# The last store of a recurrence-and-mixture kernel, cut into four uneven parts, and two pairs of stores merged

## The chip, the cores and the metric

The kernel runs on one core of one Trainium2 chip. Its time is the device time of one execution in microseconds (us). The core has a tensor engine (PE, with its weight loads shown as PEld), a vector engine (DVE), a scalar engine (ACT), GpSimd (POOL), a sync engine (SP) that here only issues DMAs, and 16 DMA engines that move the data.

## The reference

Two layers follow each other. The first is a gated recurrence over 5056 tokens for 4 sequences of 256 channels; the second is a soft mixture of 8 experts with 4 slots each, over all 4 x 5056 = 20224 tokens.

```python
# x, f_logit: (4, 5056, 256) f32; lower_bound: (256,)
f = lower_bound + (1 - lower_bound) * sigmoid(f_logit)
for t in range(S):
    h = f[:, t] * h + (1 - f[:, t]) * x[:, t]
    y[:, t] = h
x = y.reshape(B * S, D)
# phi: (256, 32); w1: (8, 256, 1024); w2: (8, 1024, 256)
logits = x @ phi
d = softmax of logits over all tokens        # dispatch
slot_input = d.T @ x                         # 32 x 256
slot_out[e] = relu(slot_input[e] @ w1[e]) @ w2[e]
c = softmax of logits over the 32 slots      # combine
out = c @ slot_out                           # (20224, 256) f32
```

The output has 20.7 MB. No row of it can be computed before `slot_out` is there, and that needs all tokens.

## The kernel before

The kernel has three stages. Until about 130 us it streams `f_logit` and `x` through the recurrence in groups of 512 tokens and keeps the exponentials of the logits (`etall`, slots on the partitions) and the slot sums. Until 143 us the experts' two products give `slot_out` and `slot_bd` (two copies of it, each masked for one of two sequences). Then the output stage combines and stores.

In the output stage the tokens of a sequence are cut into blocks: two of 2048 tokens and one of 896 (`blocks`; `end = len(blocks) - 1` is the index of the small one), and 64 left-over tokens. Within a block, partition p holds n_r tokens in a row (16 or 7), so that a partition's part of a store is contiguous in the output: 16 tokens of 1 KB are one run of 16 KB. `whole` (L786) computes one sequence's block by itself. `couple` (L801) computes a block for the two sequences 2j and 2j + 1: for each token position r one matmul (L811) with `slot_bd` into PSUM, then a scaling by 1 / row sum that moves it into the tile `ob`, on ACT (L816) where r % 7 is 1, 4 or 6 and on DVE (L819) otherwise. When the positions up to one of `ends` are done, they are stored through SP's queue: either both sequences in one DMA (`both`, L828) or one DMA for each (L831). `rest` (L835) does the left-over tokens.

The order of the stage is written out by hand at the end (L853 to L862): sequence 3's first block in four stores, the small block for sequences 0 and 1 (`couple(end, 0, (4, 7))`) and for 2 and 3 (`couple(end, 1)`), sequence 2's first block, the left-over tokens, and then three couples of large blocks: `couple(0, 0)`, `couple(1, 0)`, `couple(1, 1)`. Each of these six sequences' blocks is a store of 128 partitions x 16 KB = 2048 KB. The last one, sequence 3's second block, is the last store of the kernel.

The stores stand in SP's program in that order, and SP issues each when the results that it stores are there. Each DMA on SP's queue also takes one of eight semaphores in turn, so an issue waits for the landing of the DMA eight before it. DMAs on GpSimd's queue have semaphores of their own. In the expert stage that queue carries the weights; in the output stage GpSimd does nothing after the two `slot_bd` instructions (L747). The tile `phi_f` (L68), which the change writes to, is loaded at L81 and read by `phi_constants` (L117) near the start.

Of the kernel before, what the change touches and what calls it, by code (L numbers as in the profile page):

```python
# [18 lines left out]
def kernel(  # L19
# [10 lines left out]
    nc = tc.nc  # L30
    B, S, D = x.shape
# [4 lines left out]
    P = 128  # L36
# [31 lines left out]
    phi_f = consts.tile([P, DC, NS], F32, name="phi_f")  # L68
# [95 lines left out]
    with tc.tile_pool(name="sp2", bufs=3) as sp2, \  # L164
# [324 lines left out]
        for n in range(n_unit):  # L489
# [16 lines left out]
            else:  # L506
                end = n >= n_unit - 6
# [108 lines left out]
    with tc.tile_pool(name="ew", bufs=1) as ew, \  # L616
# [36 lines left out]
        for q in range(E // Q):  # L653
# [4 lines left out]
            if q == 0:  # L658
                nc.tensor.matmul(cs_ps, rep2, cs1, start=True, stop=True)
                src = ht_ps.rearrange("p f (j s) -> p f j s", s=NS)[:, :, :, ds(0, SPE)]  # L660
                src = bass.AP(tensor=src.tensor, offset=src.offset,
                              ap=[list(src.ap[0]), [P, FC], [NS + SPE, Q], [1, SPE]])
                dst = hid[:, :, :, ds(0, SPE)]
                dst = bass.AP(tensor=dst.tensor, offset=dst.offset,
                              ap=[list(dst.ap[0]), [Q * NS, FC], [NS + SPE, Q], [1, SPE]])
# [4 lines left out]
            for j in range(Q):  # L670
                s0 = (Q + j) * SPE
                src = ht_ps[:, :, ds(j * NS + s0, SPE)]
# [33 lines left out]
        for j in range(Q):  # L706
# [30 lines left out]
            if j == 1:  # L737
                row_sums(25, n_grp * R)
                q = n_grp * R - 1
                k = ds(wide_r * B, (q - wide_r) * B + B // 2)  # L740
# [7 lines left out]
        for r in range(DIR):  # L748
# [3 lines left out]
            else:  # L752
# [3 lines left out]
                out=out[ds((B - 1) * S, P * wide_r)].rearrange(  # L756
                    "(p r) d -> p r d", r=wide_r)[:, r], in_=begun[:, r])
# [3 lines left out]
    with tc.tile_pool(name="osb", bufs=3, reuse_waits="tile") as osb:  # L761

        def by_vector(ob, op, scale):
            nc.vector.tensor_tensor(ob, op, scale.broadcast_to(list(ob.shape)), ALU.mult)  # L764

        def by_scalar(ob, op, scale):
            for i in range(ob.shape[1]):
                nc.scalar.activation(ob[:, i], op[:, i], ACT.Copy, scale=scale[:, i])

        def share(op, i, b, r, k):  # L770
            t0, n_r = blocks[i]
            ew = etall[ds(b * NS, NS), ds(t0, P * n_r)].rearrange("s (p r) -> s p r", r=n_r)
            for j in range(k):
                nc.tensor.matmul(op[:, j], ew[:, :, r + j], slot_out[ds(b * NS, NS)],  # L774
                                 start=True, stop=True, skip_group_check=True)

        def scale_of(i, b, r, k):
            return rrow[:, ds(blocks[i][0] // P + r, k), ds(b, 1)]

        def rows_of(i, b):  # L780
            t0, n_r = blocks[i]
            return out[ds(b * S + t0, P * n_r)].rearrange("(p r) d -> p r d", r=n_r)

        pout = ctx.enter_context(tc.tile_pool(name="pout", bufs=8, space=PSUM, reuse_waits="tile"))

        def whole(i, b, pieces, ends):  # L786
            n_r = blocks[i][1]
            dst = rows_of(i, b)
            ob = osb.tile([P, n_r, D], F32, name="ob", tag="ob")
            done = pieces[0][1]  # L790
            for j, r, k in pieces:
                op = pout.tile([P, 2, D], F32, name="op", tag="op")
                share(op, i, b, r, k)
                (by_vector, by_scalar)[j](ob[:, ds(r, k)], op[:, ds(0, k)],
                                          scale_of(i, b, r, k))
                if r + k in ends:
                    q = ds(done, r + k - done)
                    nc.sync.dma_start(out=dst[:, q], in_=ob[:, q])
                    done = r + k

        def couple(i, j, ends=()):  # L801
            t0, n_r = blocks[i]
            ends = ends or (n_r,)
            ew = etall[ds(j * 2 * NS, 2 * NS), ds(t0, P * n_r)].rearrange(
                "s (p r) -> s p r", r=n_r)
            scale = rrow[:, ds(t0 // P, n_r), ds(2 * j, 2)]
            ob = osb.tile([P, 2, n_r, D], F32, name="oc", tag="oc")
            done = 0
            for r in range(n_r):
                op = pout.tile([P, 2, D], F32, name="op", tag="op")  # L810
                nc.tensor.matmul(op.rearrange("p u d -> p (u d)"), ew[:, :, r],  # L811
                                 slot_bd[ds(j * 2 * NS, 2 * NS)].rearrange("s u d -> s (u d)"),
                                 start=True, stop=True, skip_group_check=True)
                if r % 7 in (1, 4, 6):
                    for u in range(2):
                        nc.scalar.activation(ob[:, u, r], op[:, u], ACT.Copy,  # L816
                                             scale=scale[:, r, ds(u, 1)])
                else:
                    nc.vector.tensor_tensor(  # L819
                        ob[:, :, r], op,  # L820
                        scale[:, r].unsqueeze(2).broadcast_to([P, 2, D]), ALU.mult)
                if r + 1 in ends:
                    q = ds(done, r + 1 - done)
                    if done or i == end and ends == (n_r,):
                        both = out[ds(2 * j * S, 2 * S)].rearrange(
                            "(u t) d -> u t d", u=2)[:, ds(t0, P * n_r)].rearrange(
                            "u (p r) d -> p u r d", r=n_r)
                        nc.sync.dma_start(out=both[:, :, q], in_=ob[:, :, q])  # L828
                    else:
                        for u in range(2):  # L830
                            nc.sync.dma_start(out=rows_of(i, 2 * j + u)[:, q],  # L831
                                              in_=ob[:, u, q])
                    done = r + 1

        def rest():  # L835
            n_p = B // 2
            ob = osb.tile([P, n_p, D], F32, name="ob", tag="ob")
            dst = out.rearrange("(b t) d -> t b d", b=B)
            for j in range(n_p):
                k = ds(j * 2 * NS, 2 * NS)  # L840
                op = pout.tile([P, 2, D], F32, name="op", tag="op")
                nc.tensor.matmul(op.rearrange("p u d -> p (u d)"),
                                 left[k].rearrange("s t u -> s (t u)"),
                                 slot_bd[k].rearrange("s u d -> s (u d)"),
                                 start=True, stop=True, skip_group_check=True)
                nc.scalar.copy(ob[:, j], op[:, 0])
                nc.vector.tensor_tensor(ob[:, j], ob[:, j], op[:, 1], ALU.add)
            by_vector(ob, ob, rrow[:, n_grp * R - 1, ds(0, n_p)].unsqueeze(2))
            for j in range(n_p):
                nc.sync.dma_start(out=dst[ds(S - L, L), ds(2 * j, 2)], in_=ob[:, j])  # L850

        end = len(blocks) - 1
        whole(0, B - 1, ((0, 2, 1), (1, 3, 1), (0, 4, 2), (1, 6, 2), (0, 8, 2),  # L853
                         (1, 10, 2), (0, 12, 2), (1, 14, 2)), (4, 6, 10, 16))
        couple(end, 0, (4, 7))
        couple(end, 1)
        whole(0, B - 2, [(t % 2, 2 * t, 2) for t in range(wide_r // 2)], (wide_r,))
        rest()
        for i in range(end):
            for j in range(B // 2):  # L860
                if i or j < B // 2 - 1:
                    couple(i, j)  # L862
# [30 lines left out]
```

## Time and profile before

| what | value |
|---|---|
| median of 3 runs | 197.45 us (197.3 to 197.46) |
| the profiled execution | 197.19 us, its span 195.4 us |
| busy: PE, DVE, ACT, POOL | 80%, 75%, 72%, 53% of the span |
| bytes read from HBM, written to it | 58.23 MB, 20.71 MB |
| first store issued | 143.60 us |
| last store: issued, last landing | 176.96 us, 194.50 us |
| stores of 2048 KB from L831: issue to landing, median of the six | 13.1 us |

The span runs from the first to the last instruction of the profiled execution; the time of the execution is a little longer than its span. A DMA is split into packets, one for each contiguous run, which the DMA engines work off in order; each engine ends its share with a 4-byte packet that steps the semaphore. Landing times are those of these steps. The trace gives start, duration, size and queue of each packet, but not the number of the DMA engine.

### The profile page before, as it was taken

How to read it: one execution, taken by the hardware profiler on the slowest of the kernel's cores; microseconds unless marked ns; L12 is line 12 of the kernel's file. 1: busy time of each engine (PE TensorE's matmuls, PEld its weight loads, DVE VectorE, ACT ScalarE, POOL GpSimd, SP SyncE). 2: the span in 40 equal slices, each digit the busy share in tenths (PEclk: the TensorE clock that was granted, in tenths of full speed). 3: DMA queues.
4: the chain of work that ended last, by engine and by line, in shares of the span. 5: the costliest groups of instructions: out<-in, count | busy, mean ns of one | idle time of the engine just before them, and what ended most of it. 6: DMA issues, size and time to landing. Idle time of an engine off the chain costs nothing.

```text
span 195.4 us, 3269 instructions
## 1 busy us (share of the span) xinstructions
PE 155.5 (80%) x1204; PEld 106.2 (54%) x1204; DVE 146.9 (75%) x188; ACT 140.0 (72%) x194; POOL 103.7 (53%) x80
## 2 busy tenths in 40 slices
PE   5768888999979879889797887999999999990000
PEld 4446666776767757668586575567874433320000
DVE  2679797999797999999999999815189798770000
ACT  3688698799788998989987597545279987771000
POOL 2589578874996879874979969384030000000000
PEclk9999999999997999999999999999995555555555
DMA  5999999999999999999999999999949999999995
GB/s 206 421 419 418 431 424 426 428 428 355 376 426 423 429 317 421 429 416 346 363 420 419 260 211 214 215 214 215 166 150 424 424 454 429 429 429 429 429 429 218
DMA packets 14274, 70.75 MB, mean 362 GB/s; under 512 B 1570, under 2 KB 2851, under 8 KB 10291
## 3 DMA queue, kind: packets, MB, share of 16 engines
q1 hardware_dynamic: 11632, 62.13, 76.6%
q0 software_dynamic: 2624, 8.42, 21.6%
q8 instruction: 9, 0.15, 0.3%
q14 instruction: 7, 0.05, 0.1%
q10 hardware_dynamic: 2, 0.00, 0.0%
HBM read 58.23 MB, written 20.71 MB: 404 GB/s over the span
## 4 chain that ended last, share of the span: by engine, by line
PE 33%; DVE 24%; DMA 15%; ACT 8%; issue 7%; POOL 3%; ACTq 0%; SPq 0%; DVEq 0%; POOLq 0%
DVE h L318 18%; DMA x_t<-in_x_dram 15%; PE op L811 11%; DVE ht L348 4%; PE hp L331 4%; POOL u_t L247 3%; ACT oc L816 3%; PE up L272 2%; ACT a L300 2%; PE op L774 2%; PE so_ps L712 2%; PE sp L262 2%; PE lg L362 2%; PE tail L396 1%; PE slot_ps L413 1%
## 5 line engine op out<-in xcount | busy, mean ns | idle before, releaser
L247 POOL TENSOR_TENSOR u_t<-s_t,x_t 128x1024 bf16<-128x1024 bf16 (+1 forms) x39 | 82.5, 2127 | 23.5 <-ACT s_t L236 11.1
L318 DVE TENSOR_TENSOR_SCAN h<-a,h,up 128x512 bf16<-128x512 f32 (+1 forms) x72 | 86.5, 1251 | 6.1 <-PE up L272 5.0
L236 ACT ACTIVATE s_t<-f_t 128x2048 bf16<-128x2048 f32 (+2 forms) x23 | 38.3, 1669 | 6.0 <-DMA f_t<-in_f_logit_dram 3.7
L331 PE MATMUL hp<-base,h 128*128 128x128 f32 (+1 forms) x160 | 29.1, 305 | 10.2 <-DVE ht L348 8.1
L331 PEld LDWEIGHTS hp<-base,h 128*128 128x128 f32 (+1 forms) x160 | 22.6, 207 | 20.0 <-DVE ht L348 12.7
L811 PE MATMUL op<-slot_bd,etall 64*128 64x512 bf16 x62 | 26.2, 596 | 0.8 <-DVE ob L764 0.2
L300 ACT ACTIVATE a<-sp,lbs 128x1024 f32<-128x1024 bf16 x24 | 25.4, 1113 | 1.5 <-PE sp L262 1.0
L816 ACT ACTIVATE oc<-op,rrow 128x256 f32<-128x256 f32 x54 | 22.2, 490 | 4.5 <-PE op L811 4.3
L819 DVE TENSOR_TENSOR oc<-op,rrow 128x512 f32<-128x512 f32 x35 | 22.3, 684 | 3.0 <-PE op L811 2.9
L184 PE MATMUL slot_ps<-base 128*128 128x256 f32 x72 | 23.1, 429 | 0.0
L262 PE MATMUL sp<-base,s_t 128*128 128x128 f32 x144 | 20.6, 285 | 3.1 <-ACT a L307 2.1
L307 ACT ACTIVATE a<-sp,lbs 128x512 f32<-128x512 bf16 (+2 forms) x22 | 17.8, 858 | 3.8 <-PE sp L262 3.5
L262 PEld LDWEIGHTS sp<-base,s_t 128*128 128x128 f32 x144 | 16.9, 147 | 6.1 <-ACT a L307 3.9
L272 PE MATMUL up<-base,u_t 64*128 64x64 f32 x192 | 18.1, 232 | 1.2 <-POOL u_t L247 1.0
L811 PEld LDWEIGHTS <-etall 64*128 64x128 bf16 x62 | 9.2, 152 | 16.7 <-issue 11.5
L272 PEld LDWEIGHTS up<-base,u_t 64*128 64x128 f32 x192 | 14.2, 140 | 5.9 <-POOL u_t L247 2.6
L348 ACT COPY ht<-hp 128x512 f32<-128x512 f32 (+1 forms) x18 | 10.5, 582 | 8.2 <-PE hp L331 8.1
L348 DVE COPY ht<-hp 128x512 f32<-128x512 f32 (+1 forms) x22 | 14.7, 668 | 0.8 <-PE hp L331 0.8
L184 PEld LDWEIGHTS slot_ps<-base 128*128 128x128 f32 x72 | 12.6, 205 | 2.5 <-issue 1.1
L318 DVE TENSOR_TENSOR_SCAN h<-a,up 128x512 bf16<-128x512 f32 x8 | 9.4, 1210 | 2.0 <-PE up L262 1.9
L362 PE MATMUL lg<-h,phi 128*32 128x512 bf16 (+1 forms) x80 | 9.6, 389 | 0.0
L262 PE MATMUL up<-base,u_t 128*128 128x128 f32 x48 | 7.8, 282 | 1.3 <-POOL u_t L247 1.1
(124 smaller groups left out, 147.5 us busy)
## 6 DMA issues: line engine op xcount, KB each, us to landing
f_t<-in_f_logit_dram SPq DMA_DIRECT2D x12, 1024.0 KB, 12.2
x_t<-in_x_dram SPq DMA_DIRECT2D x12, 1024.0 KB, 11.4
out_dram<-oc SPq DMA_DIRECT2D x6, 2048.0 KB, 13.1
w_sb<-in_moe_w_dram POOLq DMA_DIRECT2D x14, 512.0 KB, 9.8
f_t<-in_f_logit_dram SPq DMA_DIRECT2D x12, 512.0 KB, 8.5
x_t<-in_x_dram SPq DMA_DIRECT2D x12, 512.0 KB, 8.8
out_dram<-ob SPq DMA_DIRECT2D x1, 2048.0 KB, 10.2
out_dram<-oc SPq DMA_DIRECT2D x1, 1792.0 KB, 8.3
```

Source lines behind the costliest of these rows:

```text
L184: nc.tensor.matmul(slot_bank[:, 1], ident_f, wide_ident, start=False, stop=False, skip_group_check=True)
L236: nc.scalar.activation(s_t, f_t, ACT.Sigmoid, scale=-1.0)
L247: nc.gpsimd.tensor_tensor(uts[n][:, :r], s_t[:, :r], x_t[:, :r], ALU.mult)
L262: nc.tensor.transpose(ps[:, :, r], t[:, r], ident_f)
L272: nc.tensor.transpose(v[:, :, r], t(r)[k].bitcast(F32), ident_f[k, k])
L300: nc.scalar.activation(a, sp[:, :, :, :, o], ACT.Identity, scale=nomlb[:, ds(o, 1)], bias=1.0)
L318: nc.vector.tensor_tensor_scan(h[:, :T, o], decays[n // 2, o][:, n % 2, :T], up[:, :T, o], hs[number(g - 1, b)][:, ds(used(g - 1) - 1, 1), ...
L331: nc.tensor.transpose(hp[:n_p, r], hw[:, :n_p, r], ident_f)
L348: copy(hts[g][:n_p, b].rearrange("p r d -> p (r d)").bitcast(F32), hps.pop(n)[:n_p].rearrange("p r c -> p (r c)"))
L811: nc.tensor.matmul(op.rearrange("p u d -> p (u d)"), ew[:, :, r], slot_bd[ds(j * 2 * NS, 2 * NS)].rearrange("s u d -> s (u d)"), start=Tru ...
L816: nc.scalar.activation(ob[:, u, r], op[:, u], ACT.Copy, scale=scale[:, r, ds(u, 1)])
L819: nc.vector.tensor_tensor(ob[:, :, r], op, scale[:, r].unsqueeze(2).broadcast_to([P, 2, D]), ALU.mult)
```

## The change

In `couple` the condition for storing both sequences in one DMA is widened. The small block's first part (sequences 0 and 1, four tokens a partition) and the block of `couple(0, 0)` are now one DMA each instead of two: 128 x 2 runs of 4 KB, and 128 x 2 runs of 16 KB.

The last store, 128 partitions x 16 KB, is issued by a new function `uneven` in four parts: partitions 0 to 111, 112 to 115 and 116 on SP's queue, and 117 to 127 on GpSimd's queue. Ahead of the latter, GpSimd's queue gets a load of 5 x 2 numbers of `moe_phi` into `phi_f`, which nothing reads afterwards.

```diff
+        def uneven(dst, src):
+            a = P - 16
+            mark = phi_f.rearrange("p o s -> p (o s)")[:5, ds(0, 2)]
+            nc.gpsimd.dma_start(out=mark, in_=moe_phi[ds(0, 5), ds(0, 2)])
+            nc.gpsimd.dma_start(out=dst[ds(a + 5, 11)], in_=src[ds(a + 5, 11)])
+            for k in (ds(0, a), ds(a, 4), ds(a + 4, 1)):
+                nc.sync.dma_start(out=dst[k], in_=src[k])
+
         def couple(i, j, ends=()):
...
                 if r + 1 in ends:
                     q = ds(done, r + 1 - done)
-                    if done or i == end and ends == (n_r,):
+                    if done or i == end or i + j == 0:
                         both = out[ds(2 * j * S, 2 * S)].rearrange(
...
                         nc.sync.dma_start(out=both[:, :, q], in_=ob[:, :, q])
                     else:
                         for u in range(2):
-                            nc.sync.dma_start(out=rows_of(i, 2 * j + u)[:, q],
-                                              in_=ob[:, u, q])
+                            dst, src = rows_of(i, 2 * j + u)[:, q], ob[:, u, q]
+                            if i == end - 1 and 2 * j + u == B - 1:
+                                uneven(dst, src)
+                            else:
+                                nc.sync.dma_start(out=dst, in_=src)
                     done = r + 1
```

The order of the DMAs on SP's queue is otherwise as before, and the work of PE, DVE and ACT is the same. GpSimd's program gets its two DMAs behind the `slot_bd` instructions.

## The prediction

> **What bounds the kernel now.** I read the page from the top: busy shares, the forty slices, the queues; then the stages, SP's waits, the end of the timeline and the packets of single moments. The slices come first (DMA share in tenths, then GB/s; one slice is 4.9 us):
>
> ```profile
> DMA  5999999999999999999999999999949999999995
> GB/s 206 421 419 418 431 424 426 428 428 355 376 426 423 429 317 421 429 416 346 363 420 419 260 211 214 215 214 215 166 150 424 424 454 429 429 429 429 429 429 218
> ```
>
> From the 31st slice (146.6 us) the DMA engines are full, at 424 to 454 GB/s, until the last one. The tail by stages (busy time of each engine, PE clock, DMA share, GB/s):
>
> ```profile
> 146.60:154.00 7.40, 7.40 (x28) 3.65 (x26) 6.71 (x11) 7.37 (x20) 0.00 (x0) 0.50 1.03 421
> 154.00:180.00 26.00, 21.48 (x48) 7.09 (x46) 18.79 (x30) 18.38 (x45) 0.00 (x0) 0.50 1.02 434
> 180.00:193.40 13.40, 0.00 (x0) 0.00 (x0) 0.00 (x0) 0.00 (x0) 0.00 (x0) 0.50 0.97 417
> ```
>
> After 180 no compute engine works and the stores alone run. The end of the timeline, and SP's waits:
>
> ```profile
> 176.04 0.84 ACT L816 ACTIVATE oc<-op,rrow 128x256 f32<-128x256 f32 x2 [0.24 <-PE op L811]
> 176.54 1.62 SPq L831 DMA_DIRECT2D out_dram<-oc  x2
> ...
> SPq L888 <- DMA out_dram<-oc: 15.8, 4, 4.8
> ```
>
> The last store is issued at 176.96 and SP waits 15.8 us for landings. So the tail is bytes over bandwidth, and whatever leaves one DMA engine with more to do than the rest. The packets of the last moment (from 193.415 us):
>
> ```profile
> DMA packets 2, 0.02 MB, mean 21 GB/s; under 512 B 1, under 2 KB 1, under 8 KB 1
> q1 hardware_dynamic: 2, 0.02, 4.9%
> ```
>
> One 16 KB packet and its 4-byte semaphore packet: one engine alone. A store of 128 rows of 16 KB is 128 packets, eight on each of 16 engines, 611 ns each and 607 from start to start. Fifteen engines end their last data packet between 193.28 and 193.42, the sixteenth at 194.03. Their semaphore steps land from 193.62 to 193.76, and the late one at 194.50; the closing barrier takes 0.93 more, to 195.43.
>
> Where the lateness comes from: of the 507 packets of 16 KB that start between 160 and 180, 29 take 614 to 639 ns instead of 611, about one in a round of 16, so one engine; the excess sums to 0.42 us. Of the 342 later ones none is long. In the landings the late engine's gap grows from 0.06 us (store landed 151.7) to 0.75 (179.98), then stays there. It grows while instructions run and stops within three microseconds of the last one.
>
> **The sum's base.** The profiled execution took 197.19 us: span 195.43 and 1.76 around it. The median of the runs is 197.45, 0.26 above; I carry a difference found in the span over to the median.
>
> **Part by part.** *The two merged pairs.* The first pair holds SP for 1.45 us (332 and 1022 ns); stores of the merged form took 1082 and 747 ns (L828), so SP gains 0.4 to 0.7. The store ahead, issued at 146.60, lands at 150.42, so the engines have work until about 150 and see none of it; the second pair is issued at 161.42 while the store of 154.23 is under way until 164.38. Packets and bytes stay. Cost 0; without that cover, a late start of up to 1.1 us each.
>
> *The small unread load.* Issued on POOL behind the last `slot_bd` (ends 145.30): issue 0.59 us (the weight loads' figure), five runs of 8 bytes, 4-byte packets took 9 to 25 ns. Its buffer is last read at 7.2 us (L117). Under 0.05 us on an engine, in a stretch where the engines aren't yet full. Cost 0, at most 0.05.
>
> *Eleven rows on GpSimd's queue.* They wait, as SP's store did, for the last ACT and DVE results (176.88), then 0.59 us of issue. Behind them on POOL stands only the closing barrier, which SP reaches at 194.6. Each is one more packet in a round of the engines' work; the nearest rows are that queue's weight packets (8 KB read, 4 KB written) at 324 ns against 309 for 8 KB on SP's queue, so eleven engines could pay some 0.03 us. The end of the sum doesn't depend on when these packets go, only on which engine carries them.
>
> *Three issues on SP.* The last issue took 1.20 us; three of at most 1.2 end by 180.6, and the store ahead of them lands at 188.9 to 189.7. Each waits also for the store eight before it; the latest of those lands at 164.77. Cost 0, with eight microseconds of cover.
>
> *Who carries what.* This decides. 112 rows are 7 packets on each engine. If the other 16 rows stay whole packets, 4 + 1 + 11 of them fall on 16 engines: an engine that gets none (the relief) means another that gets two, hence nine in all. Nine packets end 0.607 us after 193.28 to 193.42, at 193.89 to 194.03: where the late engine ends today. So in whole packets the relief is worth nearly nothing. The question is whether the one row is split. The one row of the trace with a single run is the load of `lower_bound` (1 KB, one partition):
>
> ```profile
> DMA packets 2, 0.00 MB, mean 10 GB/s; under 512 B 1, under 2 KB 2, under 8 KB 2
> q10 hardware_dynamic: 2, 0.00, 3.3%
> ```
>
> One data packet and one semaphore packet, so one engine. The new row is 16 tokens of 1 KB in the kernel, but contiguous on both sides, and the built program holds it as one run of 16 KB. I take one packet; the other end, 16 packets of 1 KB (46 ns each in the trace), stays in the range.
>
> The Trainium skill, "DMA: Bandwidth & Descriptors", section "Why a DMA increments its semaphore by 16 and not by 1", says that a DMA uses the largest number of engines up to 16 that divides its slowest dimension, on SP's path the lowest-numbered ones, on GpSimd's consecutive ones from a round-robin cursor. By it the five-run load moves the cursor past engine 4, the eleven rows take engines 5 to 15, the four rows 0 to 3, and a row that is one run engine 0 again: engine 0 has nine packets, engine 4 seven. The `lower_bound` packets agree for one run; nothing here shows 4, 5 or 11 rows.
>
> *The size.* In the profiled execution: the nine-packet engine lands at 193.89 to 194.03 plus 0.35 to 0.47 (what lay between data end and landing), 194.24 to 194.50, against 194.50: 0.00 to -0.26, say -0.1. But that credits the change with 0.6 us of lateness that a recorded execution shows and that stops with the instructions. What slows those packets the trace doesn't say; the records of instructions are one thing that stops then, and timed executions may not write them. The nearest rows of full queues without it are the stores after 180 (excess 0) and the loads from 7 to 26 us, where the last landing trails the next by a steady 0.12 to 0.16. With 0.1 of lateness to relieve, nine packets against eight cost 0.607 - 0.1 = 0.5.
>
> **The cases.** *A, the forecast (0.30): nine packets decide.* The timed executions have under 0.2 us of lateness, or the nine-packet engine is the late one itself; +0.45 to +0.6, taken at +0.5: 197.95. Against it: profiled and median differ by 0.26 in the wrong direction for a recording that costs time.
>
> *B (0.20): as in the profile.* Relief and ninth packet cancel: -0.26 to 0, 197.35. It holds from 0.2 us of lateness in the timed executions; below that A holds.
>
> *C (0.28), the other side: the one row is split in 16.* All engines but the relieved carry 8 1/16: 193.76 + 0.05 = 193.81; the late one, if it is the relieved one, 194.50 - 0.607 + 0.046 = 193.94. Gain 0.56: 196.89. For it: the row is sixteen tokens, and the trace has no single run above 1 KB; against it the packet above. It needs some 0.45 us of lateness in the timed executions.
>
> *D (0.15): the change doesn't do what it says; the eleven rows start at the first engine.* No DMA of fewer than 16 rows on GpSimd's queue is in the trace. Then one engine carries 7 + 1 + 1 + 1 = 10 packets: 193.42 + 1.21 + 0.35 to 0.47 = 194.98 to 195.10, +0.5 to +0.6 against the late end of the profile, +1.2 against an even one: 197.95 to 198.65. The same section of the Trainium skill notes, as an exception, GpSimd copies spread over all 16 with the rounded-up share each; by that the eleven rows sit on engines 0 to 10, which is this case.
>
> *E (0.07): the relieved engine isn't the late one.* The late one keeps eight: 0, or +0.6 where it gets the ninth; 197.45 mostly. The Trainium skill, same page, section "Latency and other measured facts", calls engines 7 and 15 usually slower, where the rule above relieves engine 4; the trace doesn't number the engines.
>
> **The numbers.** Slower by over 0.2%, 0.4 us, about what a measurement can tell: A, D and part of E, 0.48. Within it: B and most of E, 0.24. Faster: C, 0.28. The forecast is A's 197.95, its own range 197.85 to 198.1. C on one side and A and D on the other must both be inside, so the range goes from 196.8 to 198.2; the upper end of D is left out.
>
> **What would show it.** Right: after the last common packet round, one engine with one more 16 KB packet, issued by the one-row store, which lands last; 16 KB packets in number as before (896); a gap of one landing to the rest of 0.6 us. C would show 1024-byte packets, 16 more, and 895 of 16 KB, with the last landings within 0.2 us. D would show two lone packets in a row. Wrong altogether: a DMA gap between 147 and 165 (the merged stores), or a last store issued after 188.

## The result, and the profile after

The changed kernel takes 203.59 us (median of 5 runs, 202.98 to 204.19) against 197.3 before: 6.3 us slower, ratio 1.0316 with a 95% interval of 1.0291 to 1.0341. The forecast was 197.95, 0.5 above the 197.45 of the runs at hand then, with a range of 196.8 to 198.2. The direction was right and the size wrong by more than a factor of ten. The profiled execution took 202.98 us, span 201.2.

The forty slices of the page after (DMA share in tenths, GB/s; a slice is 5.0 us):

```profile
DMA  6999999999999999999999999999399999999991
GB/s 210 419 424 419 432 417 435 423 425 324 415 427 425 375 370 422 425 408 307 414 423 323 223 213 213 214 212 195 98 401 430 442 417 420 463 420 257 414 303 72
```

The DMA engines stay at nine tenths up to the 39th slice, but in the 37th, 39th and 40th slices they move 257, 303 and 72 GB/s; before, 429 held up to the last one. The tail by stages (busy time of each engine, PE clock, DMA share, GB/s; a packet counts where it starts, so a share can pass 1):

```profile
154.00:180.00 26.00, 21.46 (x48) 7.04 (x46) 18.79 (x30) 18.35 (x45) 0.53 (x1) 0.50 1.02 431
...
182.00:188.00 6.00, 0.00 (x0) 0.00 (x0) 0.00 (x0) 0.00 (x0) 0.00 (x0) 0.50 1.04 303
188.00:194.00 6.00, 0.00 (x0) 0.00 (x0) 0.00 (x0) 0.00 (x0) 0.00 (x0) 0.50 1.00 355
194.00:199.00 5.00, 0.00 (x0) 0.00 (x0) 0.00 (x0) 0.00 (x0) 0.00 (x0) 0.50 0.57 200
```

Until 180 nearly all is as before (431 against 434 GB/s from 154 on). From 182 to 194 the DMA share is 1.00 and more while the rate falls to 303 and 355: the engines aren't idle, their packets take longer. SP's wait at the end grew accordingly, from 15.8 us to

```profile
SPq L899 <- DMA out_dram<-oc: 19.3, 4, 7.3
```

behind issues that now last until 180.5 instead of 178.2.

The packets say which. The eleven rows on GpSimd's queue start between 182.1 and 182.8, right after the packets under way, five microseconds after their issue at 177.14. They take 0.97 to 4.12 us each where 0.611 was expected, 2.98 on average. The queues of the stretch from 182 to 183 (packets, MB, time that they took, as a share of 16 engines):

```profile
q0 software_dynamic: 16, 0.18, 205.1%
q1 hardware_dynamic: 15, 0.25, 66.2%
```

The first line is GpSimd's queue: the eleven rows and five 4-byte packets that start in this microsecond take 2.05 x 16 = 32.8 us in all. Between 182 and 188, 24 packets of 16 KB are over 640 ns. In the same moments three engines' packets on SP's queue take 1.2 to 1.4 us, one after another. The last whole store but one, which used to land at 184.82, lands at 188.45; the next at 195.84 instead of 189.68. From 188 on come the rest of the last whole store, the 112 rows, the four and the one: 192 packets of 16 KB, 50 of them over 640 ns, up to 2449; the 112 rows land last, at 200.15. Of the 391 packets of 16 KB that start on SP's queue after 178, 63 are over 640 ns; the excess over 611 adds up to 31 us on that queue and to 26 on GpSimd's.

### The profile page after: what moved, and what is told of

It reads as the page before. It is cut to its first block, busy times and chain, and to the rows that moved or that the text cites. A ratio compares the mean times of both kernels' runs of the same rounds, so it can differ in the third digit from the quotient of the medians.

```text
span 201.2 us, 3269 instructions
## 1 busy us (share of the span) xinstructions
PE 155.4 (77%) x1204; PEld 106.2 (53%) x1204; DVE 146.9 (73%) x188; ACT 140.0 (70%) x194; POOL 104.8 (52%) x82
## 4 chain that ended last, share of the span: by engine, by line
issue 23%; DMA 22%; DVE 20%; PE 12%; ACT 7%; POOL 3%; SPq 0%; POOLq 0%; ACTq 0%; DVEq 0%
DVE h L318 15%; DMA w_t<-in_moe_w_dram 8%; DMA f_t<-in_f_logit_dram 8%; DMA w_sb<-in_moe_w_dram 6%; PE hp L331 4%; DVE ht L348 3%; POOL u_t L247 3%; PE sp L262 3%; PE up L272 2%; ACT a L300 2%; ACT s_t L236 2%; ACT a L307 1%; PE lg L362 1%; DVE ob L764 1%; DVE et L386 1%
## 5 line engine op out<-in xcount | busy, mean ns | idle before, releaser
L805 POOL DMA_DIRECT2D out_dram<-oc x1 | 0.5, 526 | 31.3 <-ACT oc L824 31.3
```

## The experiments

Theory 1, formed on these packets: neighbouring partitions share a way out of SBUF that one engine alone fills, and a store of all 128 partitions is dealt out so that every engine has a way of its own. The Trainium skill, "SBUF — State Buffer", section "Door 1: The DMA port swizzle (why `[64,N]` ≈ `[32,N]`)", has such a rule: 16 ports, four neighbouring partitions and the four that stand 32 further on behind each. Rows 117 to 127 then lie behind three ports, which fits the three slowed engines; 3, 4 and 4 rows, and the packets of the engine that belongs there, share each. Rival 2: GpSimd's queue is slow for stores, or slows what is beside it. Rival 3: the prediction's, that only the number of packets on an engine counts.

**Each shape alone** (`probe`). The four stores of sequences 0 to 3's second blocks give way to a list of single stores with a vector copy between two, which waits for the landing and writes into what the next one reads (an excerpt; the expectation speaks of three stores left out, the kernel leaves out four):

```diff
...
+            for e, a, n, step in ((sy, 0, 128, 1), (sy, 0, 112, 1), (sy, 0, 64, 1), (sy, 0, 16, 1),
+                                  (sy, 0, 8, 1), (sy, 0, 8, 4), (sy, 0, 4, 1), (sy, 0, 4, 4),
+                                  (gp, 0, 8, 1), (gp, 0, 8, 4), (gp, 117, 11, 1), (sy, 117, 11, 1),
+                                  (gp, 0, 128, 1)):
+                k = slice(a, a + n * step, step)
+                e.dma_start(out=dst[k], in_=src[k])
+                nc.vector.tensor_copy(ob[:, 1, :, ds(0, 1)], ob[:, 0, :, ds(0, 1)])
...
```

> The last three stores of 2 MB are left out (their rows stay unwritten); in their place 13 stores out of the last tile run one after the other, each alone, since a small vector operation between two of them writes into what both read. Rows of 16 KB, in order: on SP's queue 128 rows, 112, 64, 16, 8 neighbouring, 8 at every fourth partition, 4 neighbouring, 4 at every fourth; on GpSimd's queue 8 neighbouring, 8 at every fourth, 11 (117 to 127); on SP's queue the same 11; on GpSimd's 128. Theory 1 (neighbouring partitions share a way out of SBUF that carries one row per 0.61 us, four partitions and their partners 32 further on one way, sixteen ways in all): 128 rows 4.9 us of packets with 611 ns each; 64 rows 4.9 too, packets of 1.2 us; 16, 8 and 4 neighbouring rows 2.4 us, packets up to 2.4 us; 8 or 4 at every fourth partition 0.61; 11 rows 2.4 us on either queue; 112 rows 4.9 us or more with packets of mixed length. Rival 2 (GpSimd's queue is slow for stores, or slows what is beside it): all on SP's queue 611 ns a packet whatever the rows (112 rows 4.3 us, 64 rows 2.4, the small ones 0.61), on GpSimd's queue several microseconds, with 128 rows too. Rival 3 (only the number of packets on one engine counts, the prediction's sum): 611 ns a packet everywhere.

The kernel takes 241.71 us (one run), which only says how long the list is. DVE's copies in its timeline; the number in brackets is the idle time that the store's landing ended, so from issue to landing and a little more (the first includes waiting for the last results):

```profile
182.85 0.18 DVE L856 COPY oc<-oc 128x16 f32<-128x16 f32 x1 [6.95 <-DMA out_dram<-oc]
190.69 0.18 DVE L856 COPY oc<-oc 128x16 f32<-128x16 f32 x1 [7.66 <-DMA out_dram<-oc]
197.74 0.18 DVE L856 COPY oc<-oc 128x16 f32<-128x16 f32 x1 [6.87 <-DMA out_dram<-oc]
201.84 0.18 DVE L856 COPY oc<-oc 128x16 f32<-128x16 f32 x1 [3.92 <-DMA out_dram<-oc]
205.82 0.18 DVE L856 COPY oc<-oc 128x16 f32<-128x16 f32 x1 [3.79 <-DMA out_dram<-oc]
208.51 0.18 DVE L856 COPY oc<-oc 128x16 f32<-128x16 f32 x1 [2.51 <-DMA out_dram<-oc]
212.43 0.18 DVE L856 COPY oc<-oc 128x16 f32<-128x16 f32 x1 [3.73 <-DMA out_dram<-oc]
215.02 0.18 DVE L856 COPY oc<-oc 128x16 f32<-128x16 f32 x1 [2.40 <-DMA out_dram<-oc]
219.94 0.18 DVE L856 COPY oc<-oc 128x16 f32<-128x16 f32 x1 [4.74 <-DMA out_dram<-oc]
222.61 0.18 DVE L856 COPY oc<-oc 128x16 f32<-128x16 f32 x1 [2.49 <-DMA out_dram<-oc]
227.18 0.18 DVE L856 COPY oc<-oc 128x16 f32<-128x16 f32 x1 [4.38 <-DMA out_dram<-oc]
231.18 0.18 DVE L856 COPY oc<-oc 128x16 f32<-128x16 f32 x1 [3.82 <-DMA out_dram<-oc]
238.28 0.18 DVE L856 COPY oc<-oc 128x16 f32<-128x16 f32 x1 [6.92 <-DMA out_dram<-oc]
```

Four neighbouring rows take 3.73 us, four at every fourth partition 2.40; eight, 3.79 and 2.51. The packets, from the first one's start to the last one's end:

| rows | queue | all packets, us | one packet, ns |
|---|---|---|---|
| 128 | SP; GpSimd | 5.03; 5.03 | 608 to 641, mostly 611 |
| 112 | SP | 6.35 | 608 to 1489, over half at 608 to 616 |
| 64 | SP | 5.23 | mostly 1273 |
| 16 neighbouring | SP | 2.62 | 2116 to 2474 |
| 8 neighbouring | SP; GpSimd | 2.58; 2.57 | 2142 to 2487 |
| 8 at every fourth | SP; GpSimd | 0.67; 0.68 | 608 |
| 4 neighbouring | SP | 2.55 | 2182 to 2314 |
| 4 at every fourth | SP | 0.67 | 608 |
| 11 (117 to 127) | GpSimd; SP | 2.57; 2.56 | 900 to 2507 |

Theory 1's order holds in every row, and its figures to within 0.35 us where it gave one. For stores that stand alone rivals 2 and 3 are out: the queue makes no difference to a shape, and the packet's time goes by how many engines read behind the same four partitions and the four 32 further on. 112 rows take longer than 128. Four rows, 64 KB, in 2.55 us are 25.7 GB/s. 64 rows take as long as 128, as that rule of the Trainium skill has it.

One thing the table doesn't separate: the rows lie in the output as they lie in SBUF (`dst[k]` and `src[k]`), and no run moved one without the other. That the shared way is on SBUF's side is the rule's account and isn't shown by a run.

**The parts of the change.** The merged pairs alone (`merge_only`: `uneven` issues `dst` and `src` whole):

> The two merged pairs alone, the last store whole on SP's queue. All theories: as before, 197.3 us within 0.2. If the merged stores were part of the loss: above 198.

197.4 us, ratio 1.0006 (0.9997 to 1.0015). The merges cost nothing.

The last store in two parts on SP's queue (`sp_112_16`):

```diff
...
-            nc.gpsimd.dma_start(out=mark, in_=moe_phi[ds(0, 5), ds(0, 2)])
-            nc.gpsimd.dma_start(out=dst[ds(a + 5, 11)], in_=src[ds(a + 5, 11)])
-            for k in (ds(0, a), ds(a, 4), ds(a + 4, 1)):
+            for k in (ds(0, P - 16), ds(P - 16, 16)):
```

> The last store in two parts on SP's queue, 112 rows and 16, nothing on GpSimd's queue. Theory 1 (shared ways out of SBUF): the 112 rows are dealt out in sevens, so engines meet on the same partitions' way, and the last 16 rows share four ways: slower than before by 2 to 4 us, 199.5 to 201.5. Rival 2 (GpSimd's queue): as before, 197.3. Rival 3 (packets per engine): as before, eight packets on each engine.

198.57, ratio 1.0065 (1.0049 to 1.0082), 1.3 us slower: theory 1's direction, below its 2 to 4. In its tail the packets are long (over 0.65 us) only from 188 on.

Two tokens of every partition on GpSimd's queue behind the small load (`gp_token`):

```diff
...
+            nc.gpsimd.dma_start(out=dst[:, ds(14, 2)], in_=src[:, ds(14, 2)])
+            nc.sync.dma_start(out=dst[:, ds(0, 14)], in_=src[:, ds(0, 14)])
```

> The last store in two parts that both have all 128 partitions: 14 tokens of each on SP's queue, two tokens (256 KB, more than the eleven rows) on GpSimd's queue behind the small load. Theory 1: every engine keeps to its own partitions, so no loss: 197.3 within 0.3. Rival 2 (GpSimd's queue, or two queues at once): slower by over 2 us. Rival 3: as before.

197.53, ratio 1.0023 (1.0008 to 1.0038). More bytes than the eleven rows went the same way over GpSimd's queue, ahead of the other 14 tokens, for 0.3 us instead of 6. They went as 64 packets of 4 KB and 159 ns, though, so this run changes the packet's size along with the shape; 16 KB rows on this queue follow below.

**When the rows go.** The last store left out (`last_none`), and only the eleven rows of it stored, behind the small load (`last_gp11`); the other rows stay unwritten:

> The last store (2 MB, sequence 3's second block) is left out altogether; its rows stay unwritten. It is the base for the next kernel. All theories: eight rounds of 607 ns less, 197.3 - 4.9 = 192.4 us.

> Of the last store only the eleven rows 117 to 127 are stored, on GpSimd's queue behind the small load as in the change; the other 117 rows stay unwritten. The eleven packets go while the two stores ahead are under way. If they jam the three ways out of SBUF that they share and hold up their engines' other packets (theory 1): the store under way lands 3 to 4 us late as in the changed kernel (188.45 there), and the time is 192.4 + 3 to 3.5 = 195.4 to 196. If each costs only its own packet (the prediction): 192.4 + 0.6 at most, 193.0.

192.39 (ratio 0.9755, 0.9735 to 0.9774) and 196.07 (0.9941, 0.9921 to 0.9961). The eleven rows alone cost 3.7 us, with nothing else of the last store there; the time is at the upper end of theory 1's 195.4 to 196, and the prediction's count of packets gave 193.0 at most. Up to 0.6 of that isn't theirs: the merged store of `couple(0, 0)`, which is issued long before them, began to land at 174.50 in this trace and at 173.88 in that of `last_none`. The stages of `last_gp11` (same columns as above), and below them one of `last_none`:

```profile
178.00:182.00 4.00, 0.00 (x0) 0.00 (x0) 0.00 (x0) 0.00 (x0) 0.00 (x0) 0.50 0.92 393
182.00:186.00 4.00, 0.00 (x0) 0.00 (x0) 0.00 (x0) 0.00 (x0) 0.00 (x0) 0.50 1.03 225
186.00:190.00 4.00, 0.00 (x0) 0.00 (x0) 0.00 (x0) 0.00 (x0) 0.00 (x0) 0.50 0.98 418
```

```profile
182.00:186.00 4.00, 0.00 (x0) 0.00 (x0) 0.00 (x0) 0.00 (x0) 0.00 (x0) 0.50 1.07 459
```

Four microseconds at half the rate with all engines busy: each of the eleven engines stands behind its one packet, and by theory 1 the way that belongs to it lies idle meanwhile. The packets show the standing still. About 16 of both queues are open at any moment, so an engine has one at a time; at 183.1 they are the eleven and only five of SP's queue.

To see whether it matters when the rows go, the same 112 and 16 rows as above, with the 16 on GpSimd's queue, hence ahead (`gp_16`), and the four parts of the change all on SP's queue, hence behind (`sp_parts`). The first has the small load ahead of the 16 rows, the second is without it:

```diff
# gp_16
...
+            nc.gpsimd.dma_start(out=dst[ds(P - 16, 16)], in_=src[ds(P - 16, 16)])
+            nc.sync.dma_start(out=dst[ds(0, P - 16)], in_=src[ds(0, P - 16)])
# sp_parts
...
+            for k in (ds(0, P - 16), ds(P - 16, 4), ds(P - 12, 1), ds(P - 11, 11)):
+                nc.sync.dma_start(out=dst[k], in_=src[k])
```

> As the kernel with 112 rows and 16 on SP's queue (198.57), but the 16 rows go on GpSimd's queue behind the small load. Theory 1a (rows that share few ways cost most when they cut in ahead of full queues, since each engine then stands behind its one slow packet): 4 to 7 us slower than before, 201.5 to 204. Theory 1b (it does not matter when they go): 198.6, as on SP's queue.

> The four parts of the change, 112, 4, 1 and 11 rows, all on SP's queue in this order, without the small load and without GpSimd's queue. Theory 1a: they go last, so little stands behind them: 198.3 to 200. Theory 1b, or if the four rows and the one row were the cost: 203, as the change. Rival 3 (packets per engine alone; the first engine then carries ten): 198.5.

`gp_16` takes 201.08 (1.0178, 1.0129 to 1.0227), 2.5 us more than with the 16 rows behind. Its four runs fall in two pairs, near 200.1 and 202.0, and the median is below the 201.5 to 204 of theory 1a. Its stage from 182 to 186 against that of `sp_112_16` (first line `gp_16`):

```profile
182.00:186.00 4.00, 0.00 (x0) 0.00 (x0) 0.00 (x0) 0.00 (x0) 0.00 (x0) 0.50 0.92 238
```

```profile
182.00:186.00 4.00, 0.00 (x0) 0.00 (x0) 0.00 (x0) 0.00 (x0) 0.00 (x0) 0.50 1.00 426
```

The line of `gp_16` is of a run of 201.97 us; at 182.8 all 16 open packets in it are of GpSimd's queue and none is of SP's.

`sp_parts` takes 200.5 (1.0166, 1.0151 to 1.0182), half a microsecond above what was expected, and 3.1 us less than the change with the same four shapes. About half of these 3.1 is the small load, which `sp_parts` leaves out: against the change without it (202.14, `no_mark` below) it is 1.6. So both count: the shapes, and that some go ahead. Theory 1a has the order right and missed both sizes by half a microsecond.

**Queue or rows, under load.** Eight rows on GpSimd's queue, without the small load, nothing else of the last store: rows 0, 4 to 28 (`last_gp8far`, `k = slice(0, 32, 4)`) and rows 0 to 7 (`last_gp8near`, `ds(0, 8)`).

> As the kernel with the last store left out (192.39), but eight rows of it are stored on GpSimd's queue while the stores ahead are under way: rows 0, 4, 8 to 28, no small load. Theory 1 (four neighbouring rows share a way out of SBUF): these eight have eight ways and cost one packet each on their engines, 192.4 + 0 to 0.6. Rival 2 (a store on GpSimd's queue holds up the engines that it uses, whatever its rows): 195 to 196, as the eleven rows (196.07).

> As the kernel with eight rows at every fourth partition, but rows 0 to 7. Theory 1: two ways for eight rows, each shared also with the engine that works it off anyway: 192.4 + 3 to 4 = 195.4 to 196.4. Rival 2: the same as the other eight rows. Rival 3 (packets only): 193.0 at most in both.

193.32 (ratio 0.9803, 0.9774 to 0.9831) and 194.38 (0.9856, 0.9828 to 0.9885). Far: all eight packets at 611 ns, no packet on SP's queue above 640 from then on; the time is 0.3 above the expected range. The 0.9 us over `last_none` contain 0.5 by which the merged store of `couple(0, 0)` landed later in its trace (174.35 against 173.88), so a packet's worth is left. Near: packets of 1.16 to 2.41 us, 2.0 us over `last_none` (with the same 0.5 in it), less than the 3 to 4 expected. The order is theory 1's, and rival 2 is out under load too; the size was put too high. The two engines that belong to these ways are perhaps themselves among the eight and so don't compete. The trace fits: the eight packets of SP's queue that start beside the rows around 182.0 all take 611 ns, where the change has three at 1.2 us or more. No run tests it.

**The small load** (`no_mark`: the change without its line):

> The changed kernel without the small unread load, so that the eleven rows may begin at another engine. Theory 1: the rows share the same three ways whichever engines carry them: 202 to 205, as the change (203.59). If the small load itself, or the engines it picks, were the cost: back towards 197 to 198; if it spares an engine a tenth packet: up to 0.6 slower than the change.

202.14 (1.025, 1.022 to 1.028): 1.4 us less than the change, and still 4.9 slower than before. The small load shifts the loss; it doesn't make it. How a load that was over 30 us earlier adds 1.4 us isn't shown. A shift of the eleven rows to other engines was the thought behind this run, but the traces don't bear it out: with and without the load, five engines go on with SP's packets beside the rows, and three of them are slowed to 1.2 us or more.

**The late engine** (`which`):

```diff
...
+            nc.sync.dma_start(out=dst[:, ds(0, 15)], in_=src[:, ds(0, 15)])
+            a = 0
+            for n in (2, 4, 6, 8, 10, 12, 14, 72):
+                nc.sync.dma_start(out=dst[ds(a, n), ds(15, 1)], in_=src[ds(a, n), ds(15, 1)])
+                a += n
```

> To find the late engine. The last store in nine parts on SP's queue: 15 tokens of all 128 partitions, then the sixteenth token of 2, 4, 6, 8, 10, 12, 14 and 72 partitions, 1 KB each. By the packet counts of the change (four rows: four engines; one row: one) a part of n rows runs on n engines; if these are always the first n, the parts that include the late engine land about 0.6 us after those that don't. Late engine among the first two: all parts late. Fifteenth or sixteenth: none of the small parts late, only the large one. Time: 197.3 to 198.5, since the small parts share few ways.

198.68 (one run, 0.2 above the expected range). The 15 tokens land at 193.50 and, late, at 194.22. The parts of two and four rows have no late step (last at 193.64 and 193.82, 0.11 after the one before); the part of six has (194.42, 0.42 after). If a part of n rows runs on the first n engines, the late one is the fifth or sixth, where the change would have relieved the fifth. In the larger parts the shared ways blur it. The Trainium skill, "DMA: Bandwidth & Descriptors", section "Latency and other measured facts", calls 7 and 15 usually slower, and guesses that this is particular to GpSimd's path. If the first n engines carry a part of n rows, this run on SP's queue shows another one late.

## Why the prediction was wrong, step by step

The loss of 6.3 us can be taken apart by three complete kernels. The four shapes behind everything else cost 200.5 - 197.2 = 3.3 us (`sp_parts` against before). That the eleven rows go ahead adds 202.14 - 200.5 = 1.6 (`no_mark`), and the small load 203.59 - 202.14 = 1.4. The kernels with rows left out divide it otherwise: 196.07 - 192.39 = 3.7 for the eleven rows ahead, and 2.6 more for the other 117 rows (203.59 - 196.07 = 7.5) than for the whole store in its old shape (197.25 - 192.39 = 4.9). Both sums close because each is a chain of differences; what the runs show is the size of the terms.

*The step that failed* is the one on the eleven rows: "Each is one more packet in a round of the engines' work", and "The end of the sum doesn't depend on when these packets go, only on which engine carries them." Priced at 0.611 us, the packets took 2.98 on average, and when they go is worth 1.6 us (`no_mark` against `sp_parts`), or 2.5 and 3.1 together with the small load (`gp_16` against `sp_112_16`, the change against `sp_parts`). That load, priced at 0.05 at most and worth 1.4, is the other term that failed.

The same wrong price stood under *who carries what* (112 rows as seven packets of 611 ns on each engine: 6.35 us alone instead of 4.25) and under every case: A, B, C, D and E all counted packets. The trace before holds no store of 16 KB rows with fewer than 128 partitions, so that duration was a row of another shape; a bound taken from both sides should have asked what changes when engines and partitions no longer match. The stores of the left-over tokens, from 64 partitions, would not have told: all their 256 packets of 1 KB took 46 ns on average, as those from 128 partitions did. Theory 1 doesn't cover them: two engines on a way would take some 76 ns (an estimate: 1 KB of the 16 KB that pass in 0.61 us, twice), and why they don't stays open. The Trainium skill's port rule would have told, and the prediction didn't weigh it.

*A, nine packets decide*: the direction came out by luck, not for its reason. One engine with nine packets can't be seen behind engines that are out of step by up to 6.7 us (the landing steps of the last whole store run from 189.09 to 195.84). The one row landed at 198.12, before the 112 rows, where the prediction had it last. The two signs of "wrong altogether", a DMA gap between 147 and 165 and a last issue after 188, both stayed away: neither asked for full engines at a lower rate. Neither is there any sign of how late the late engine is in executions without a trace: that stays open. In `probe`, with no instruction beside it, the store of 128 rows shows no late engine: 611 ns a packet, but for one round in which all are about 630.

*What held*: the merges cost nothing, and SP's three issues were over at 180.5, long before their turn; the one row went as one packet (896 packets of 16 KB in all, 885 on SP's queue and 11 on GpSimd's, and one landing step for it, four for the four rows), so case C was out. D's extra packet can't be told from the rest, but its placement of the eleven rows fits better than the forecast's. By theory 1 the three slowed engines are the owners of the three ways, so none of them carries one of the rows. If the engines own the partitions in order, the last three own 116 to 127; the forecast's engines 5 to 15 would include these three, D's 0 to 10 don't. The traces don't number the engines, so this stays an inference.

No version found here beats the kernel before; `merge_only` equals it.

## What to carry to other kernels

Cut a store along the free dimension, not along the partitions: with all 128 partitions the packets took 611 ns each, and with 112, 64 or 11 of them engines met on the same way out. When a DMA share stays full and the rate falls, compare packet durations with those of the same size elsewhere in the trace. An odd shape did least harm behind everything else; on a second queue it cut in ahead, and each engine that got one of its packets stood still with all that was queued behind it.

## What the runs showed of the hardware that was not expected

- A way that four neighbouring partitions share passes four 16 KB rows in 2.55 us, 0.64 us a row. On such ways 4, 8, 11 or 16 neighbouring rows take 2.55 to 2.62 us, 8 spread ones 0.67.
- GpSimd's queue is as fast as SP's for these stores (128 rows 5.03 us on both, 11 rows 2.57 and 2.56), and its packets were taken up while SP's queue was full, some five microseconds after their issue (177.14 and 182.1). The stores on it that stood alone in `probe` began 1.1 us after theirs; why it takes longer beside a full queue stays open.
- 112 rows took 26% longer than 128 (6.35 against 5.03 us).
